# Three reorderings in a fused attention, expert and dense kernel: the order of loads where expert 1 begins, where the weight decoding stands among the experts, and the order of the last sums

## The chip, the cores and the metric

The kernel runs as one program on one core of a Trainium2 chip. The metric is device microseconds per execution; lower is better. Five engines work side by side, each on an instruction stream of its own, strictly in order: TensorE (PE in the profile, with its weight loads as PEld), VectorE (DVE), ScalarE (ACT), GpSimd (POOL) and SyncE (SP). In this kernel nearly all transfers are issued from SP's stream and a few from POOL's; an engine waits for another, or for a transfer, on semaphores.

## The reference

Three stages follow each other. The first is a linear attention with decay over 4 batches, 8 heads and 768 steps; it yields a table `x` of 3072 tokens by 256. The second sends each token to one of 8 experts, and the third is a dense layer pair for all tokens:

```python
expert_idx = np.argmax(logits, axis=1)
for e in range(E):
    mask = expert_idx == e
    h = np.maximum(x[mask] @ w1[e], 0.0)            # 256 -> 1024
    out[mask] = gate_w[mask, None] * (h @ w2[e])    # 1024 -> 256
# third stage, on the experts' output
h = x @ w_in                                        # 256 -> 2048
g = h * np.cos(h)
return (g @ w_out).astype(np.float32)               # 2048 -> 256
```

`w_in` and `w_out` arrive as 64-bit numbers and must be turned into 32-bit ones on the chip.

## The kernel before, in words

**Lists.** While the attention runs, each finished token's row is scattered into a table `xs` in DRAM, behind the rows of its expert's list. A list has room for 432 rows. Behind the last row of list `e`, `fill(e)` (L868) copies a block of zeros `zd` to `xs`, so that a later read of 432 rows finds zeros there and not rubbish. `rows_of(e)` (L879) then reads the list into a tile `xg`. It can be issued only when the zeros of that list have landed.

**Experts.** The loop at L1217 runs over the experts `e` and, inside, over eight slices `f` of the hidden dimension. All products are made in 32-bit precision out of two parts of each operand, a high one and a rest (`h1`, `l1`, `h2`, `l2` of the weights, `xh`, `xl` of the rows, `hh`, `hl` of the hidden values), so that each product takes three matmuls. For each `f`, TensorE makes `ph` (six matmuls, L1233); ScalarE rounds it to `hh` (L1237); VectorE makes the rest `hl` (L1238); and three slices later TensorE takes both up again in `second` (L1201), six matmuls into `py`. So TensorE can run ahead of `hl` by three slices and no further. The last three slices are multiplied after the loop over `f`.

In the same loop stand, in an order that is written out by hand:

- `load_w1(e + 2)` and `load_w2(e + 2)` (L727 and L732): 1 MB each, from SP, into a slot that must be free;
- `split_w(e + 1)` (L756): the high part of the next expert's weights by ScalarE (L743) and the rest by POOL or VectorE (L752), in quarters of 512 columns. `g.S1` names the engine of each quarter for expert 1 alone; later experts use POOL;
- `gates(xg)` (L830) for list `e + 2`: POOL takes a power (L836), VectorE a row of small operations (L840 to L858), and one scaling of the rows (L863, L865);
- `decode()` (L1071): the 64-bit weights of the third stage, 16 pieces of 512 KB fetched one after the other (`fetch`, L1063) into two buffers `raw`. Each piece takes one operation of ScalarE (`tb`, L1084), three of VectorE (L1086, L1088, and L1092 or L1099), and for the first eight pieces one more of each (L1094, L1096). `decode` is a generator; each step of it issues about one operation. `side.take(n)` takes `n` steps: `g.TK[f]` for expert 0 and `g.TE[f]` for the others (L1245), and three more between two experts. At slice 5 of the last expert, all steps that are left are issued at once (L1247);
- `split_out` (L1104): in the last expert, the two parts of `w_out`, by ScalarE and POOL.

**The start of the expert stage.** Between attention and experts a string `g.END` gives the order of the steps that prepare lists 0 and 1. Behind it stand `overflow()` (a branch that isn't taken here), `load_w2(1)`, `fill(2)` from POOL, `rows_of(2)` from SP, and the first two `fetch`es (L1183 to L1188).

**The third stage.** Tokens are taken in blocks `n` (five of 512, two of 256), the 2048 middle columns in 16 slices `f`; a pair (n, f) is a unit. `up` makes `pu`, VectorE and ScalarE make `gh` and `gl` of it, and `down` (L1352), six units later, adds its product to `po` for each 128 tokens `j` of the block. When the last slice of a `j` is in, `finish` (L1316) copies `po` out and scatters the rows to the output, from POOL. In the last block the products of the last two slices are held back and then made for each `j` in turn (L1359 to L1361), so that the first `j` can leave while the second is still computed.

Of the kernel before, what the change touches and what calls it, by code (L numbers as in the profile page):

```python
# [20 lines left out]
NT, D, E, F, F2 = 3072, 256, 8, 1024, 2048  # L21
# [621 lines left out]
def tile_attention_moe_moe2(ctx: ExitStack, tc: tile.TileContext, A1, A2, X, BNh, BT, CT, cst_d, emb, tau, w1, w2, w_in, w_out, out):  # L643
    nc = tc.nc
    ET = mybir.EngineType
    g = G_()
# [33 lines left out]

    g.G1 = (3, 1, 2, 1, 1, 0, 0, 0)
    g.G2 = (0, 0, 0, 0, 2, 0, 2, 2)
    g.TE = (2, 1, 1, 1, 1, 1, 1, 1)
    g.TK = (0, 0, 0, 1, 0, 0, 0, 1)
    g.L2 = "vvvv"
    g.WL = 16
    g.S1 = ("vvvv", "pppp")
    g.WN = {19: 1, 20: 5, 21: 2, 22: 5}
    g.TAIL = "tltttwtwtwmrttttttlrttttwltttttwttwttttttttttt"
    g.END = "wxwcwccwcwwcwwwwwcwxwxwrxxcxxxwwxxxxgxkkgkkggxxxxxg"  # L690
    LAG = 6
    TW = [512] * 5 + [256] * 2
    T0 = [sum(TW[:n]) for n in range(len(TW))]
# [32 lines left out]
    def load_w1(e):  # L726
        r1 = raws[0].tile([128, 2048], F32, tag="r1", name="r1")  # L727
        for k in range(2):
            nc.sync.dma_start(r1[:, F * k:F * k + F], w1[e, 128 * k:128 * k + 128, :])
        W.setdefault(e, {})["r1"] = r1  # L730
# [34 lines left out]
    side = Sides()  # L765
# [102 lines left out]
    def fill(e, et=ET.SP, q=nc.sync):  # L868
        r = nc.values_load(endi[:, e + 1:e + 2], engines=[et], min_val=0, max_val=E * SX - CAP)
        i = q.dma_start(quarters(xs[bass.ds(r, CAP), :]), quarters(zd))  # L870
        for j in prev + early + loads:
            tc.declare_no_dep(i.ins, j, reason="no scatter reaches the rows behind a list's end, and the first list lies before the others")
        return i.ins
# [99 lines left out]
    with ExitStack() as actx:  # L973
        g.apool = actx.enter_context(tc.tile_pool(name="apool", bufs=1))
        g.apool2 = actx.enter_context(tc.tile_pool(name="apool2", bufs=2))
        acc = attn_router(actx, tc, g)

        pcn = g.psU.tile([1, E], F32, tag="u", name="pcn")
        nc.tensor.matmul(pcn, lhsT=g.onesb[:, 0:1], rhs=acc, start=True, stop=True)

        def counts():
            nc.vector.tensor_tensor(out=cnt[:, 1:], in0=pcn, in1=base[:, 1:], op=ALU.subtract)
            yield
            nc.vector.tensor_tensor_scan(out=off, data0=ones[:, :NL], data1=cnt, initial=0.0, op0=ALU.mult, op1=ALU.add)
            yield
            nc.vector.tensor_tensor(out=off, in0=off, in1=cnt, op=ALU.subtract)
            nc.vector.tensor_tensor(out=endi, in0=cnt, in1=base, op=ALU.add)
            fills.append(fill(1, ET.Pool, nc.gpsimd))
            yield
            nc.vector.tensor_copy(cnti, off)  # L990
            xg.append(rows_of(1))

            over = cp.tile([1, NL], F32, name="over")
            nc.vector.tensor_tensor(out=over, in0=cnt, in1=capf, op=ALU.subtract)
            yield
            nc.vector.tensor_scalar(novs, over, 127.0, 0.0, op0=ALU.add, op1=ALU.max)
            yield
            nc.vector.tensor_scalar(novs, novs, 7, None, op0=ALU.arith_shift_right)
            yield
            with nc.allow_low_precision(reason="whole numbers below 2^24"):  # L1000
                nc.vector.tensor_reduce(nov, novs, axis=AX.X, op=ALU.add)

        xg, fills = [], []
        def next_list():
            carved = Carved(few)
            numbers(0, g.xg0, carved)
            yield
            yield from gates(xg[0], carved, g.GE)

        steps = dict(w=g.window, c=counts(), x=second_list(), g=next_list())  # L1010
        for op in g.END:
            if op == "r":
                load_w1(1)
            elif op == "k":
                g.keep_warm(1)
            else:
                next(steps[op], None)
        for op in "xwc":
            for _ in steps[op]:
                pass  # L1020
        xg, = xg
# [8 lines left out]
    with ExitStack() as mctx:  # L1030
# [151 lines left out]

        overflow()  # L1183
        load_w2(1)
        fill(2, ET.Pool, nc.gpsimd)
        xs_ = {1: xg, 2: rows_of(2)}
        numbers(1, xg, mp2, ET.Pool, nc.gpsimd)
        raw_ = [fetch(0), fetch(1)]  # L1188
        x_ = g.x0
        gt = [steps["g"], None]  # L1190
        side.add(decode())
# [25 lines left out]
        for e in range(E):  # L1217
            w = {k: W[e][k].rearrange("p (a b) -> p a b", a=2 if k[1] == "1" else 8) for k in ("h1", "l1", "h2", "l2")}
            xh, xl = x_
            n = wide(e)  # L1220
# [7 lines left out]
            for f in range(8):  # L1228
# [11 lines left out]
                if f >= 3:  # L1240
                    q = f - 3
                    hh, hl = hs.pop(q)
                    for m in range(2):
                        second(py, m, q, w, hh, hl)
                side.take(g.TK[f] if e == 0 else g.TE[f])  # L1245
                if (e, f) == (E - 1, 5):
                    side.drain()  # L1247
                if f == 0 and 0 < e < E - 2:
                    xs_[e + 2] = rows_of(e + 2)
                if f == 2 and e + 3 < E:  # L1250
# [46 lines left out]
    with ExitStack() as zctx:  # L1297
# [30 lines left out]
        NF = F2 // 128  # L1328
# [23 lines left out]
        def down(u):  # L1352

            n, f = units[u]
            nb = TW[n] // 128
            per = 1 if n else 2
            if f == 0:
                PO[n] = [psB.tile([128, 2, D], F32, tag="po", name="po")[:, :per] for _ in range(0, nb, per)]
            last = n == len(TW) - 1 and f >= NF - 2  # L1359

            fs = [] if last and f == NF - 2 else [f - 1, f] if last else [f]  # L1361
            for j in range(nb if fs else 0):
                s = slice(128 * j, 128 * j + 128)
                po, i = PO[n][j // per], j % per
# [17 lines left out]
        for u in range(len(units) + LAG):  # L1382
            ends = LAG <= u < len(units) and units[u - LAG][1] == NF - 1
            if u < len(units):
                n, f = units[u]
# [68 lines left out]
```

## Time and profile before

| | |
|---|---|
| runs | 586.79, 586.77, 585.42 us; median 586.77 us |
| the profiled execution | 587.23 us, of which the span from its first to its last instruction is 585.6 us |
| TensorE's granted clock, mean over the span | 0.978 |
| busy | PE 94%, DVE 76%, POOL 54%, ACT 51% |
| the chain that ended last | PE 56%, DVE 8%, transfers 4%, POOL 3%, ACT 2% |

The attention ends near 140 us, the experts run from there to 306 us, and the third stage from there to the end. A busy TensorE is not TensorE at its peak, since matmuls overlap and their ends are modelled; idle time of another engine costs nothing by itself.

### The profile page before, as it was taken

The numbers are of one execution on the slowest core, as the hardware profiler recorded it, in microseconds if no ns is written. First come the engines' busy times: TensorE is split into PE (matmuls) and PEld (weight loads), VectorE is DVE, ScalarE is ACT, GpSimd is POOL, SyncE is SP. The second block draws the span as 40 slices with busy tenths as digits, with TensorE's granted clock in tenths as the row PEclk, the third lists the DMA queues.
The fourth block names the chain that finished last, engine by engine and source line by source line (L and its number), as shares of the span: only waits on it lengthen the run. The fifth ranks groups of instructions, "written<-read, shape, count | busy, mean of one in ns | idle before, by whom it ended". The sixth has DMA issues, their size and how long they took to land.

```text
span 585.6 us, 11047 instructions
## 1 busy us (share of the span) xinstructions
PE 551.4 (94%) x4000; PEld 502.1 (86%) x4000; DVE 443.3 (76%) x876; ACT 297.6 (51%) x637; POOL 314.1 (54%) x345
## 2 busy tenths in 40 slices
PE   7698999979789999999979999999999999999994
PEld 5587887878788999989968999999999999999994
DVE  5899999847787998787648977767777677776882
ACT  5163533534457566657554645445446445445562
POOL 4323543462456584566633746746745745845763
PEclk9899999999989999999979999999999999999998
DMA  8899895127676665752211000100100100100000
GB/s 202 221 218 220 206 244 166 40 93 224 232 180 240 195 194 179 244 171 81 72 37 1 2 1 1 36 2 1 38 0 1 38 1 1 38 1 9 30 20 18
DMA packets 28993, 57.00 MB, mean 97 GB/s; under 512 B 7216, under 2 KB 16056, under 8 KB 28184
## 3 DMA queue, kind: packets, MB, share of 16 engines
q1 hardware_dynamic: 26184, 47.77, 29.2%
q0 software_dynamic: 2752, 8.51, 4.4%
q8 instruction: 32, 0.52, 0.4%
q14 instruction: 25, 0.20, 0.1%
HBM read 48.50 MB, written 11.07 MB: 102 GB/s over the span
## 4 chain that ended last, share of the span: by engine, by line
PE 56%; DVE 8%; DMA 4%; POOL 3%; issue 3%; ACT 2%; POOLq 0%; SPq 0%; ACTq 0%; DVEq 0%
PE po L1373 22%; PE pu L1339 22%; PE ph L1233 6%; PE py L1203 6%; DMA xg<-xs 2%; DVE hl L1238 2%; POOL gl L1410 1%; POOL l L752 1%; DVE lg L840 1%; DVE xg L863 1%; DVE ta L1092 1%; DVE ta L1088 1%; ACT hh L1237 1%; DMA r<-in_w 1%; DMA raw<-in_w_out 1%
## 5 line engine op out<-in xcount | busy, mean ns | idle before, releaser
L1410 POOL TENSOR_TENSOR gl<-gg,gh 128x512 fp32r<-128x512 f32 (+1 forms) x111 | 125.9, 1140 | 106.4 <-PE pu L1339 63.2
L1400 ACT ACTIVATE cc<-ff,half 128x512 f32<-128x512 f32 (+1 forms) x112 | 74.4, 665 | 129.2 <-DVE ff L1398 123.3
L1396 DVE TENSOR_SCALAR tt<-pu 128x512 f32<-128x512 f32 (+1 forms) x110 | 67.4, 613 | 64.9 <-PE pu L1339 62.3
L1373 PE MATMUL po<-h,gl 128*128 128x256 f32 x384 | 108.2, 282 | 0.0
L1373 PE MATMUL po<-l,gh 128*128 128x256 f32 x384 | 108.2, 282 | 0.0
L1373 PE MATMUL po<-h,gh 128*128 128x256 f32 x382 | 107.6, 282 | 0.0
L752 POOL TENSOR_TENSOR l<-r,h 128x512 fp32r<-128x512 f32 x52 | 72.4, 1406 | 45.5 <-ACT h L743 45.1
L1373 PEld LDWEIGHTS po<-h,gh 128*128 128x128 f32 x382 | 72.3, 189 | 3.6
L1373 PEld LDWEIGHTS po<-l,gh 128*128 128x128 f32 x384 | 72.6, 189 | 3.1
L1373 PEld LDWEIGHTS po<-h,gl 128*128 128x128 f32 x384 | 73.0, 190 | 0.1
L1398 DVE SCALAR_TENSOR_TENSOR ff<-tt,pu 128x512 f32<-128x512 f32 (+1 forms) x110 | 67.0, 609 | 3.8
L1339 PE MATMUL pu<-yh,il 128*128 128x512 f32 (+1 forms) x192 | 68.5, 357 | 0.0
L1339 PE MATMUL pu<-yh,ih 128*128 128x512 f32 (+1 forms) x192 | 68.2, 355 | 0.0
L1339 PE MATMUL pu<-yl,ih 128*128 128x512 f32 (+1 forms) x192 | 68.0, 354 | 0.0
L1406 DVE SCALAR_TENSOR_TENSOR gg<-pu,cc 128x512 f32<-128x512 f32 (+1 forms) x110 | 66.7, 606 | 0.4 <-ACT cc L1400 0.4
L1409 ACT CAST gh<-gg 128x512 fp32r<-128x512 f32 (+1 forms) x112 | 60.9, 544 | 0.4 <-DVE gg L1406 0.3
L1238 DVE SCALAR_TENSOR_TENSOR hl<-ph,hh 128x432 fp32r<-128x432 f32 (+1 forms) x64 | 36.7, 577 | 24.0 <-ACT hh L1237 23.9
L1203 PE MATMUL py<-hl,h 128*128 128x432 f32 (+1 forms) x128 | 46.5, 363 | 7.8 <-DVE hl L1238 7.7
L1203 PE MATMUL py<-hh,h 128*128 128x432 f32 (+1 forms) x128 | 45.8, 358 | 2.1 <-ACT hh L1237 2.1
L1237 ACT ACTIVATE hh<-ph 128x432 fp32r<-128x432 f32 (+1 forms) x64 | 32.8, 512 | 27.8 <-PE ph L1233 27.5
L1203 PE MATMUL py<-hh,l 128*128 128x432 f32 (+1 forms) x128 | 46.0, 359 | 0.0
L1233 PE MATMUL ph<-xl,h 128*128 128x432 f32 x112 | 40.7, 363 | 0.8 <-DVE xl L1055 0.8
(220 smaller groups left out, 1205.6 us busy)
## 6 DMA issues: line engine op xcount, KB each, us to landing
r<-in_w SPq DMA_DIRECT2D x32, 512.0 KB
ac<-acd SPq DMA_DIRECT2D x10, 512.0 KB
raw<-in_w_in SPq DMA_DIRECT2D x8, 512.0 KB
raw<-in_w_out SPq DMA_DIRECT2D x8, 512.0 KB
xg<-xs SPq DMA_DIRECT2D x7, 462.4 KB
xs<-zd SPq DMA_DIRECT2D x5, 462.4 KB
XB<-in_X SPq DMA_DIRECT2D x8, 256.0 KB
bt<-in_BT SPq DMA_DIRECT2D x6, 256.0 KB
```

The lines of the kernel that those rows point to most:

```text
L752: (nc.vector if engines[q] == "v" else nc.gpsimd).tensor_tensor(out=l[:, s], in0=W[e][rn][:, s], in1=h[:, s].bitcast(F32), op=ALU.subtract)
L1203: nc.tensor.matmul(py[m][:, :b_.shape[1]], lhsT=a_[:, q, 128 * m:128 * m + 128], rhs=b_, start=q == 0 and k == 0, stop=q == 7 and k == 2)
L1233: nc.tensor.matmul(ph[:, :n], lhsT=a_[:, c, 128 * f:128 * f + 128], rhs=b_[:, c], start=k == 0, stop=k == 5)
L1238: nc.vector.scalar_tensor_tensor(out=hl, in0=ph[:, :n], scalar=0.0, in1=hh.bitcast(F32), op0=ALU.max, op1=ALU.subtract)
L1339: nc.tensor.matmul(PU[u], lhsT=a_[:, c, 128 * f:128 * f + 128], rhs=b_[:, c], start=c == 0 and k == 0, stop=c == 1 and k == 2)
L1373: nc.tensor.matmul(po[:, i], lhsT=a_[:, s], rhs=b_, start=first and per == 1, stop=q == NF - 1 and k == 2 and i == per - 1)
L1396: nc.vector.tensor_scalar(tt, pu, 0.25, MAGIC, op0=ALU.add, op1=ALU.add)
L1398: nc.vector.scalar_tensor_tensor(out=ff, in0=tt, scalar=-MAGIC, in1=pu, op0=ALU.add, op1=ALU.subtract)
L1400: nc.scalar.activation(cc, ff, AF.Sin, bias=half, scale=-TWO_PI)
L1406: nc.vector.scalar_tensor_tensor(out=gg, in0=pu, scalar=TWO_PI, in1=cc, op0=ALU.mult, op1=ALU.mult)
L1409: nc.scalar.copy(gh, gg)
L1410: (nc.vector if u >= len(units) else nc.gpsimd).tensor_tensor(out=gl, in0=gg, in1=gh.bitcast(F32), op=ALU.subtract)
```

## The change

It has five edits. `fill(2)` moves from behind `overflow()` and `load_w2(1)` to a place inside the string `g.END` (the new letter `f`), still on POOL. The first two `fetch`es move ahead of `rows_of(2)`. Two of the four quarters of `l2` of expert 1 go from POOL to VectorE (`g.S1`). The steps of `decode` are given for each expert: as before in experts 0 to 4, three more in expert 5, seven more in expert 6, two per slice in expert 7, and no drain at slice 5. In the last block of the third stage, four slices are held back, and no longer two.

```diff
-    g.TE = (2, 1, 1, 1, 1, 1, 1, 1)
-    g.TK = (0, 0, 0, 1, 0, 0, 0, 1)
+
+    g.TE = [(0, 0, 0, 1, 0, 0, 0, 1)] + [(2, 1, 1, 1, 1, 1, 1, 1)] * 4 + [(2, 2, 1, 1, 2, 1, 1, 2)] + [(2, 2, 2, 2, 2, 2, 2, 2)] * 2
     g.L2 = "vvvv"
     g.WL = 16
-    g.S1 = ("vvvv", "pppp")
+    g.S1 = ("vvvv", "vpvp")
...
-    g.END = "wxwcwccwcwwcwwwwwcwxwxwrxxcxxxwwxxxxgxkkgkkggxxxxxg"
+    g.END = "wxwcwccwcwwcwwwwwcwxwxwrxxfcxxxwwxxxxgxkkgkkggxxxxxg"
...
+            elif op == "f":
+                fills.append(fill(2, ET.Pool, nc.gpsimd))
...
         overflow()
         load_w2(1)
-        fill(2, ET.Pool, nc.gpsimd)
+        raw_ = [fetch(0), fetch(1)]
         xs_ = {1: xg, 2: rows_of(2)}
         numbers(1, xg, mp2, ET.Pool, nc.gpsimd)
-        raw_ = [fetch(0), fetch(1)]
...
-                side.take(g.TK[f] if e == 0 else g.TE[f])
-                if (e, f) == (E - 1, 5):
-                    side.drain()
+                side.take(g.TE[e][f])
...
-            last = n == len(TW) - 1 and f >= NF - 2
+            last = n == len(TW) - 1 and f >= NF - 4
 
-            fs = [] if last and f == NF - 2 else [f - 1, f] if last else [f]
+            fs = [] if last and f < NF - 1 else [f - 3, f - 2, f - 1, f] if last else [f]
```

SP's stream where the expert stage begins, before (`r` is `w2` of expert 1, `xg` the rows of list 2, `raw` the 64-bit weights, `zd` the zeros that `fill(3)` copies, and the last `r` is `w1` of expert 2):

```order
L735 DMA r_2282<-in_w 128x4x256 x2
L883 DMA xg<-xs 108x1096
L1066 DMA raw<-in_w_in 128x1024 x2
L870 DMA xs<-zd 16x7398
L729 DMA r_2418<-in_w 128x1024 x2
```

The same place in the changed kernel:

```order
L735 DMA r_2293<-in_w 128x4x256 x2
L1068 DMA raw<-in_w_in 128x1024 x2
L883 DMA xg<-xs 108x1096
L870 DMA xs<-zd 16x7398
L729 DMA r_2418<-in_w 128x1024 x2
```

The two pieces of 64-bit weights now stand ahead of the rows of list 2, and nothing else in this stream moved.

VectorE's stream from the end of expert 0 to the first `hl` of expert 1, before (`lg` to `r` and `dl` are the gates of list 2, `ta` the first decoded piece; rows of 128x256 are expert 0's):

```order
L1238 SCALAR_TENSOR_TENSOR hl<-ph,hh 128x256 x2
L1055 TENSOR_TENSOR xl<-px,xh 128x864
L1238 SCALAR_TENSOR_TENSOR hl<-ph,hh 128x256
L840 TENSOR_TENSOR lg<-xg 108x32
L842 TENSOR_REDUCE mx<-lg 108x4
L844 TENSOR_TENSOR lg<-lg,mx 108x32
L846 TENSOR_SCALAR r<-r 108x4
L848 RECIPROCAL r<-r 108x4
L850 TENSOR_TENSOR dl<-lg,r 108x32
L1086 TENSOR_SCALAR ta<-tb 128x512
L1088 SCALAR_TENSOR_TENSOR ta<-tb,ta 128x512
L1092 SCALAR_TENSOR_TENSOR ta<-raw,ta 128x512
```

The same stretch after (its first row stands between the first two `hl` of the rows above):

```order
L752 TENSOR_TENSOR l_2468<-r_2293,h_2466 128x512
L1239 SCALAR_TENSOR_TENSOR hl<-ph,hh 128x256
L1057 TENSOR_TENSOR xl<-px,xh 128x864
L1239 SCALAR_TENSOR_TENSOR hl<-ph,hh 128x256
L840 TENSOR_TENSOR lg<-xg 108x32
L842 TENSOR_REDUCE mx<-lg 108x4
L844 TENSOR_TENSOR lg<-lg,mx 108x32
L846 TENSOR_SCALAR r<-r 108x4
L848 RECIPROCAL r<-r 108x4
L752 TENSOR_TENSOR l_2468<-r_2293,h_2466 128x512
L850 TENSOR_TENSOR dl<-lg,r 108x32
L1088 TENSOR_SCALAR ta<-tb 128x512
```

Two quarters of `l2` of expert 1 have come in, one before the rows of list 2 are needed and one behind them.

VectorE's stream in the last expert from its fourth `hl`, before (`wof` is the decoded `w_out`; the last two `hl` are those of slices 6 and 7):

```order
L1238 SCALAR_TENSOR_TENSOR hl<-ph,hh 128x432 x3
L1086 TENSOR_SCALAR ta<-tb 128x512
L1088 SCALAR_TENSOR_TENSOR ta<-tb,ta 128x512
L1099 SCALAR_TENSOR_TENSOR wof<-raw,ta 128x512
L1086 TENSOR_SCALAR ta<-tb 128x512
L1088 SCALAR_TENSOR_TENSOR ta<-tb,ta 128x512
L1099 SCALAR_TENSOR_TENSOR wof<-raw,ta 128x512
L1086 TENSOR_SCALAR ta<-tb 128x512
L1088 SCALAR_TENSOR_TENSOR ta<-tb,ta 128x512
L1099 SCALAR_TENSOR_TENSOR wof<-raw,ta 128x512
L1238 SCALAR_TENSOR_TENSOR hl<-ph,hh 128x432 x2
```

The whole of the last expert after:

```order
L1239 SCALAR_TENSOR_TENSOR hl<-ph,hh 128x432
L1088 TENSOR_SCALAR ta<-tb 128x512
L1239 SCALAR_TENSOR_TENSOR hl<-ph,hh 128x432
L1090 SCALAR_TENSOR_TENSOR ta<-tb,ta 128x512
L1101 SCALAR_TENSOR_TENSOR wof<-raw,ta 128x512
L1239 SCALAR_TENSOR_TENSOR hl<-ph,hh 128x432 x2
L1088 TENSOR_SCALAR ta<-tb 128x512
L1090 SCALAR_TENSOR_TENSOR ta<-tb,ta 128x512
L1239 SCALAR_TENSOR_TENSOR hl<-ph,hh 128x432
L1101 SCALAR_TENSOR_TENSOR wof<-raw,ta 128x512
L1239 SCALAR_TENSOR_TENSOR hl<-ph,hh 128x432 x3
```

Of the nine decoding operations ahead of `hl` 6 and 7 none is left there. Expert 7 has six in all, spread ahead of its sixth `hl`; before it had twelve. The other six stand in experts 5 and 6.

## Rows read from the trace of the kernel before

**Rows 1.** Stages, windows view: length, busy of PE, PEld, DVE, ACT, POOL, clock.

```profile
117.00:140.30 23.30, 19.05 (x180) 17.76 (x176) 13.20 (x59) 8.06 (x23) 11.34 (x21) 1.00 0.44 148
160.00:182.00 22.00, 18.44 (x87) 16.87 (x88) 18.08 (x33) 12.52 (x25) 12.18 (x11) 0.84 0.69 196
240.60:261.00 20.40, 19.44 (x104) 18.30 (x103) 17.09 (x27) 12.55 (x25) 12.48 (x10) 1.00 0.54 180
261.00:281.00 20.00, 20.00 (x108) 19.20 (x108) 14.87 (x23) 12.02 (x25) 11.67 (x8) 1.00 0.31 104
281.00:306.30 25.30, 21.65 (x97) 20.03 (x96) 14.15 (x22) 13.58 (x25) 11.89 (x8) 0.88 0.19 63
```

**Rows 2.** PE, timeline: a wait in the attention, and one in expert 1.

```profile
123.87 0.73 PE L252 MATMUL pt<-IE,yT 128*128 128x136 f32 x4 [2.22 <-ACT yT L242]
...
163.08 0.73 PE L1203 MATMUL py<-hl,h 128*128 128x432 f32 x1 [4.74 <-DVE hl L1238]
```

**Rows 3.** DVE, timeline: the gates of list 2 and the first `hl` of expert 1.

```profile
153.94 0.19 DVE L840 TENSOR_TENSOR lg<-xg 108x32 f32<-108x32 f32 x1 [3.07 <-DMA xg<-xs]
...
154.39 5.81 DVE L844 TENSOR_TENSOR lg<-lg,mx 108x32 f32<-108x32 f32 x1
...
162.43 0.60 DVE L1238 SCALAR_TENSOR_TENSOR hl<-ph,hh 128x432 fp32r<-128x432 f32 x1
```

**Rows 4.** POOL, timeline: list 1's power, `fill(2)`, and expert 1's `l2`.

```profile
137.50 1.13 POOL L836 TENSOR_TENSOR few<-xg,pw 108x4 f32<-108x4 f32 x1 [1.90 <-DMA xg<-xs]
140.08 0.58 POOL L870 DMA_DIRECT2D xs<-zd  x1 [1.46 <-SPq L1121]
...
155.17 4.98 POOL L752 TENSOR_TENSOR l<-r,h 128x512 fp32r<-128x512 f32 x4
```

**Rows 5.** ACT, timeline: the first decoding operation.

```profile
155.16 0.67 ACT L1084 ACTIVATE tb<-raw 128x512 f32<-128x512 f32 x1 [4.78 <-DMA raw<-in_w_in]
```

**Rows 6.** SP, timeline of issues: expert 1's start, and expert 4's (`fill` follows its rows).

```profile
139.41 0.95 SPq L735 DMA_DIRECT2D r<-in_w  x2
149.52 0.37 SPq L883 DMA_DIRECT2D xg<-xs  x1
...
160.18 0.95 SPq L735 DMA_DIRECT2D r<-in_w  x2
...
199.75 0.93 SPq L735 DMA_DIRECT2D r<-in_w  x2
...
209.26 0.55 SPq L870 DMA_DIRECT2D xs<-zd  x1
```

**Rows 7.** Chain that ended last, in order of time: start, length, what.

```profile
161.24 9.09 DMA xg<-xs
...
280.92 4.67 PE ph L1233 x24
...
293.43 3.27 DMA raw<-in_w_out
...
300.90 5.41 PE py L1203 x14
```

**Rows 8.** PE, timeline: its two waits in the last expert.

```profile
298.45 0.47 PE L1203 MATMUL py<-hh,h 128*128 128x432 f32 x1 [1.67 <-ACT hh L1237]
300.90 0.73 PE L1203 MATMUL py<-hl,h 128*128 128x432 f32 x1 [1.98 <-DVE hl L1238]
```

**Rows 9.** Last block: PE, then DVE's last `gl`, then POOL's scatters.

```profile
574.69 0.28 PE L1373 MATMUL po<-h,gh 128*128 128x256 f32 x1
...
577.45 0.28 PE L1373 MATMUL po<-h,gl 128*128 128x256 f32 x1
...
575.27 0.43 DVE L1410 TENSOR_TENSOR gl<-gg,gh 128x256 fp32r<-128x256 f32 x1 [0.53 <-ACT gh L1409]
...
577.70 0.99 POOL L1321 DMA_INDIRECT out<-so,pidx  x1 [2.37 <-ACT so L1318]
...
578.99 0.96 POOL L1321 DMA_INDIRECT out<-so,pidx  x1 [0.21 <-issue]
```

## The prediction, made before the changed kernel was run

> **What bounds the kernel now.** I read the stages first, then TensorE's waits, then the chain of waits at these places, and last the streams of the engines that are waited for. In a plain expert stretch TensorE is busy for all of its time (20.00 of 20.00 us from 261 us on) at the full granted clock. Two stretches fall out of this: the one from 160 us with a granted clock of 0.84, and the last expert's, with 0.88 and 21.65 of 25.30 us busy [rows 1]. TensorE's longest waits of the expert stage lie there too: 4.74 us in expert 1 [rows 2], and 1.67 and 1.98 us in expert 7 [rows 8].
>
> **Place A, the start of expert 1.** SP issues `w2` of expert 1 at 139.41 us and the rows of list 2 only at 149.52 [rows 6], because the zeros behind that list, issued by POOL at 140.08, must land first [rows 4]. The rows are there at 153.94, when VectorE's `lg` ends its wait for them [rows 3]. The first piece of 64-bit weights, issued behind the rows, lets ScalarE go on at 155.16, after 4.78 us of idling [rows 5]. On VectorE the reader should see one row: the subtraction of L844, as small as the 0.19 us sum before it, takes 5.81 us and ends at 160.20 [rows 3]. POOL's run of four quarters of `l2` ends at 160.15 [rows 4]. So VectorE stands still until POOL's run is over. From there to the end of the first `hl` of expert 1 (162.43 plus 0.60) are 2.83 us, and 0.05 us later TensorE goes on. The clock adds to it: 0.84 over 22.00 us means 7.0 us at the 1.2 GHz level; 3.1 us of these TensorE was still waiting, and of the other 3.9 it lost half, 1.95 us. Place A costs 4.74 + 1.95 = 6.7 us.
>
> **Place B, expert 7.** It runs from 280.92 to 306.31 (300.90 plus 5.41), 25.4 us. Its 96 matmuls at the pace of its first 24 (4.67 us [rows 7]) take 18.7. The 6.7 us between are the two waits (3.65) and the clock (0.12 of 25.30, 3.0). The cause stands in the chain: the last piece of 64-bit weights is issued at 293.43, lands 3.27 us later [rows 7], and the decoding behind it stands ahead of the last two `hl` on VectorE.
>
> **The change, part by part.** Times are for the profiled execution, 587.23 us with its 585.6 us of span.
>
> **Zeros earlier.** The zeros of list 2 may not overwrite what the read of list 1 still takes, so POOL can issue them when list 1's rows are in, at 137.50, where its power now starts [rows 4]: 2.6 us earlier. Queued behind them on POOL are a copy and the power of list 1, which start later by 0.8 us (0.58 of issue [rows 4] and some 0.2 of address). SP's store of list 1's numbers waits for the copy, so `w2` moves from 139.41 to 140.3. I cost the delay at nothing, since expert 0's own work covers it; without that cover it is 0.8 us. The zeros took 9.4 us; if they take as long again, they land at 146.9.
>
> **Raw weights ahead of the rows.** ScalarE's 4.78 us of idling goes. But the rows now stand behind 2 MB instead of 1. The nearest row is expert 4's start, with `w2`, one piece, rows in this order: issued from 199.75, all in by 209.26 [rows 6], 9.5 us for 2.0 MB. With a second piece it is 2.5 MB, or 11.9 us, and the rows of list 2 land at T = 152.2 instead of 153.94. Bounds: 149.8 if the second piece costs nothing; 156.0 if the zeros land at 146.9 and the rows then take the 9.09 us that those of list 3 took [rows 7]. I take 152.2, because it comes from the same mix of transfers.
>
> **Two quarters to VectorE.** POOL's run after the rows is then a power (1.13 [rows 4]), a small copy (0.2) and two quarters of 1.25: 3.8 us, where it was 6.2. The first quarter on VectorE hides in its 3.07 us of idling before `lg` [rows 3]. The second stands on the path and costs 0.7 (an `hl` of 432 columns takes 0.60 [rows 3]; this one has 512). So `hl` ends at T + 3.8 + 0.7 + 2.83 = 159.5, and TensorE goes on 3.5 us earlier than at 163.08. What is left of its wait, which began at 158.3, is about 1.2 us, or 1.7 since ScalarE no longer holds back the matmul before it. The nearest wait in size, 2.22 us [rows 2], lies in a stretch with clock 1.00 [rows 1], so I take it that the clock stays and the 1.95 us come back too: 5.4 us. What is late next are the rows of list 3. They stand behind `w2` of expert 2, which SP could issue at 160.18 [rows 6], when the last quarter freed its slot. Now it is freed at T + 4.9 = 157.1, 3.1 us earlier, with less in flight. Expert 2 can follow by 3.1 us or a little more, where TensorE could by 5.4. I take **-4.5** for place A; the bounds are 0 (the rows land at T = 156, so that `hl` ends as late as before) and -6.7 (all that place A costs).
>
> The Trainium skill, page "SBUF — State Buffer", section "Who interferes with whom", says that a VectorE instruction with two SBUF inputs and a GpSimd instruction that reads SBUF exclude each other, and that the one that issues second is blocked until the first finishes. The row agrees that they exclude each other and differs in the length: the 5.81 us reach over five POOL instructions or more, not to the end of one. By the page's wording the subtraction would be free after the power, 1.1 us behind the rows, and place A would gain all 6.7 us.
>
> **Decoding spread.** It takes nine VectorE operations and the wait for a transfer out of place B: 6.7 us. Late next is the first block of the third stage, whose parts ScalarE makes from `py` while TensorE does its last nine matmuls, now at full clock (1.8 us, no longer 3.3); I leave 0.3 us for it, so **-6.4**. In return experts 5 and 6 get about two and four of VectorE's operations of 0.4 to 0.7 us, 3.9 us at most. VectorE was busy for 17.09 of 20.40 us in expert 5 and 14.87 of 20.00 in expert 6 [rows 1], so it stays below the length of an expert, and `hl` has three slices of leeway, but some operations will stand behind a POOL run. Between 0 and 3.9 I take **+0.5**, near the low end because expert 6, which gets most, had the most room.
>
> **Last sums.** The last 24 matmuls, 0.12 us apart, run from 574.69 to 577.45. The first 128 tokens now leave six matmuls earlier, by 0.72 us, and their scatter no longer holds up the second one on POOL, which began at 578.99; it can begin 0.72 us after the old start of the first, 577.70 + 0.72 = 578.42 [rows 9]. The new order needs the last `gl` at the twelfth matmul, 576.0, and it is ready at 575.70. So **-0.55**; if `gl` came late it would be 0.
>
> Sum: -4.5 - 6.4 + 0.5 - 0.55 = -10.95, and 587.23 becomes 576.3. The profiled execution stood 0.46 us above the median of the runs (586.77), so I predict 575.8.
>
> **The rivals.**
> 1. The forecast, 573.5 to 578.5: 0.53.
> 2. The rows of list 2 come no earlier. For it: 2 MB in front of them. T near 154 leaves TensorE about 3 us of waiting, and the clock falls as it did after 3.65 us in expert 7. Place A then gives 1 us: 579 to 580.5. Chance 0.20.
> 3. VectorE becomes the bound in experts 5 and 6: the 3.9 us arrive whole, with waits for POOL on top: 579 to 582.5. Against it: the free 3.3 and 5.1 us of these stretches. Chance 0.11.
> 4. The lock ends with one instruction: place A gives 6.7: 573.6 or a little less. The 5.81 us over a whole run speak against it, and nothing in this trace for it; I keep it because one row is all that shows the long lock. Chance 0.08. The Trainium skill's page "SBUF — State Buffer", section "Who interferes with whom", speaks for it.
> 5. Slower. If the rows sink far behind the raw weights, place A loses what place B and the end give (6.45 us). That takes T + 7.3 = 163.1 + 6.45, so T = 162.2: 22 us for 2.5 MB. At T = 164.5 it is 589. Expert 4's 2.0 MB in 9.5 us speak against it. Chance 0.04. The Trainium skill, page "DMA: Bandwidth & Descriptors", section "Queues, rings and completion order", says that a queue's descriptors are consumed in ring order on each DMA engine, so rows issued last cannot pass the raw weights.
> 6. The change does not do what it says: the pieces are held by their buffers as before, at both places: within 0.3%. The streams of the changed kernel speak against it. Chance 0.04.
>
> Cases 1 to 4 are faster by more than 0.3% (1.8 us, about what a measurement of this kernel can tell from no change): 0.92. Same 0.04, slower 0.04. The range 572.5 to 581.0 holds cases 1 and 4, nearly all of 2 and half of 3: somewhat over 8 in 10.
>
> **What would show each step.** Right: SP's rows of list 2 land near 152; the subtraction of L844 takes about 3.5 us; TensorE's wait in expert 1 is under 2.5 us with no stretch at 1.2 GHz; expert 7 lasts under 19.5 us without a wait over 0.5; experts 5 and 6 keep 19.5 to 21 us; POOL's last two scatters lie 1.3 us apart or more. The prediction is wrong if the rows land after 154, if the clock falls at 160 us all the same, or if expert 5 or 6 grows by more than 1.5 us.

## The result and the profile after

The changed kernel takes 579.88 us (median of 6 runs, 577.19 to 581.36) against 585.7 for the kernel before (6 runs): ratio 0.9894, 95% interval 0.9865 to 0.9924. It is faster by some 6 us, where 11 were forecast; the time lies in the range, near its upper end.

The windows view by stage, of the changed kernel (columns as in [rows 1]):

```profile
140.30:160.00 19.70, 15.40 (x96) 14.11 (x94) 12.92 (x24) 8.35 (x19) 4.35 (x5) 0.91 0.66 206
160.00:182.00 22.00, 20.12 (x87) 18.12 (x88) 15.27 (x26) 12.20 (x26) 11.97 (x10) 0.85 0.72 196
...
260.00:282.00 22.00, 20.32 (x107) 19.01 (x106) 20.16 (x32) 13.54 (x27) 11.51 (x9) 1.00 0.42 144
282.00:300.50 18.50, 18.50 (x96) 17.75 (x95) 11.46 (x16) 12.28 (x23) 11.95 (x8) 1.00 0.09 29
```

The last expert (282 us on) is now a plain stretch: TensorE busy throughout, at full clock, where it was 0.88 before [rows 1]. The stretch from 160 us is as it was, with a granted clock of 0.85 (0.84 before). So place B came back and place A did not.

TensorE's timeline at the places of the prediction: the first matmul of expert 0, one near its end, the waits in expert 1, the first of expert 2, the start of expert 6, and the last matmul of all.

```profile
135.97 0.58 PE L1234 MATMUL ph<-il,h 128*128 128x256 f32 x2 [1.21 <-ACTq L1123]
...
149.97 0.41 PE L1204 MATMUL py<-hh,l 128*128 128x256 f32 x1
...
160.16 0.73 PE L1204 MATMUL py<-hl,h 128*128 128x432 f32 x1 [3.23 <-DVE hl L1239]
...
176.05 0.46 PE L1204 MATMUL py<-hh,h 128*128 128x432 f32 x1 [1.20 <-ACT hh L1238]
...
180.50 0.35 PE L1234 MATMUL ph<-xh,h 128*128 128x432 f32 x1
...
261.89 0.47 PE L1234 MATMUL ph<-xl,h 128*128 128x432 f32 x1 [1.55 <-DVE xl L1057]
...
571.58 0.28 PE L1372 MATMUL po<-h,gl 128*128 128x256 f32 x1
```

Expert 1's wait is 3.23 us and no longer 4.74 [rows 2], but expert 2 starts at 180.50, 44.5 us after expert 0's first matmul; before it was 39.7. That the two absolute times are alike is an accident: the attention, which the edits hardly touch, ended 4.4 us sooner in this execution (135.97, where the kernel before has 140.33). In the profiles of this study expert 0 begins anywhere from 135.6 to 141.4 us, so places are compared below by their distance from that matmul, and kernels by their timed ratios. The chip has a part in this: in the four profiles of one chip it begins at 138.8 to 141.4 us, in the six of two others at 135.6 to 137.5.

VectorE, timeline: the gates of list 2, the first `hl` of expert 1, and the landing of list 3's rows with what follows.

```profile
152.99 0.19 DVE L840 TENSOR_TENSOR lg<-xg 108x32 f32<-108x32 f32 x1 [4.10 <-DMA xg<-xs]
...
153.44 3.37 DVE L844 TENSOR_TENSOR lg<-lg,mx 108x32 f32<-108x32 f32 x1
...
159.50 0.60 DVE L1239 SCALAR_TENSOR_TENSOR hl<-ph,hh 128x432 fp32r<-128x432 f32 x1
...
169.30 0.19 DVE L840 TENSOR_TENSOR lg<-xg 108x32 f32<-108x32 f32 x1 [2.02 <-DMA xg<-xs]
169.41 0.60 DVE L1239 SCALAR_TENSOR_TENSOR hl<-ph,hh 128x432 fp32r<-128x432 f32 x1
169.92 3.69 DVE L1094 SCALAR_TENSOR_TENSOR ta<-raw,ta 128x512 uint32<-128x512 uint32 x1
```

GpSimd, timeline: the zeros and the copy behind them, the quarters of `l2` of expert 1, and the work behind list 3's rows.

```profile
135.02 0.57 POOL L870 DMA_DIRECT2D xs<-zd  x1 [2.82 <-DMA xg<-xs]
135.60 0.20 POOL L826 COPY few<-xg 128x2 f32<-128x2 f32 x1
...
154.22 2.54 POOL L752 TENSOR_TENSOR l<-r,h 128x512 fp32r<-128x512 f32 x2
...
169.41 1.00 POOL L836 TENSOR_TENSOR r<-xg,pw 108x4 f32<-108x4 f32 x1 [3.39 <-DMA xg<-xs]
170.37 0.19 POOL L826 COPY ic<-xg 108x4 f32<-108x4 f32 x1
170.51 2.55 POOL L752 TENSOR_TENSOR l<-r,h 128x512 fp32r<-128x512 f32 x2
```

SP, timeline of issues: `w2` of expert 1, the raw pieces, the rows of list 2; later `w2` of expert 2 and the rows of list 3.

```profile
137.81 1.35 SPq L735 DMA_DIRECT2D r<-in_w  x2
139.21 1.72 SPq L1068 DMA_DIRECT2D raw<-in_w_in  x2
141.22 1.49 SPq L883 DMA_DIRECT2D xg<-xs  x1
...
157.76 0.96 SPq L735 DMA_DIRECT2D r<-in_w  x2
158.83 0.57 SPq L883 DMA_DIRECT2D xg<-xs  x1
```

What the reader is to see: the rows of list 2 are issued at 141.22, right after the raw pieces, and land 11.8 us later (152.99); before, they were issued ahead of the raw pieces and took 4.4 us (149.52 to 153.94, [rows 3, 6]). The subtraction of L844 is shorter, 3.37 us for 5.81. Then the same happens once more with list 3: VectorE waits for its rows, GpSimd begins a run when they land, and VectorE's L1094 takes 3.69 us, until that run is over. TensorE's 1.20 us wait before expert 2 lies behind it.

### The profile page after: what moved, and what is told of

It is laid out like the page before. It is cut to its first block, busy times and chain, and to the rows that moved or that the text cites. A ratio compares the mean times of both kernels' runs of the same rounds, so it can differ in the third digit from the quotient of the medians.

```text
span 579.1 us, 11037 instructions
## 1 busy us (share of the span) xinstructions
PE 552.6 (95%) x4000; PEld 502.0 (87%) x4000; DVE 444.9 (77%) x878; ACT 298.0 (51%) x637; POOL 310.5 (54%) x343
## 4 chain that ended last, share of the span: by engine, by line
PE 57%; DVE 9%; DMA 4%; issue 2%; ACT 2%; POOL 1%; POOLq 0%; SPq 0%; ACTq 0%
PE po L1372 22%; PE pu L1338 22%; PE py L1204 6%; PE ph L1234 6%; DMA xg<-xs 4%; DVE hl L1239 2%; DVE ta L1090 2%; DVE xg L863 1%; POOL gl L1409 1%; DVE ta L1094 1%; ACT hh L1238 1%; DVE lg L844 1%; DVE lg L840 1%; DVE ta L1088 1%; DVE wof L1101 1%
## 5 line engine op out<-in xcount | busy, mean ns | idle before, releaser
L752 POOL TENSOR_TENSOR l<-r,h 128x512 fp32r<-128x512 f32 x50 | 69.5, 1406 | 48.7 <-ACT h L743 48.3
```

The lines of the kernel that those rows point to most:

```text
L752: (nc.vector if engines[q] == "v" else nc.gpsimd).tensor_tensor(out=l[:, s], in0=W[e][rn][:, s], in1=h[:, s].bitcast(F32), op=ALU.subtract)
```

## The experiments

Each kernel was timed beside the kernel before on the same chip. Beside the changed kernel itself (median before 585.7 us) there are three groups on different chips: "start alone" to "list 3 sooner" (median before 585.13 us), "zeros behind the copy" to "rows first, zeros back" (588.14), and the last two (584.67). So ratios are compared; a ratio need not equal the quotient of the two medians. Two ratios whose intervals reach 0.003 to either side differ clearly only from about 0.004 (2.3 us) on, an estimate from these intervals. Distances are from the one profiled execution of each, and they differ by chance too: "start alone" and the changed kernel have the same start and lie 2.4 us apart at rows 2, 2.9 us at expert 2. In this table, "rows 2" and "rows 3" are the landings of those lists after expert 0's first matmul, "expert 2" is its first matmul after the same point.

| kernel | median us | ratio, 95% interval | rows 2 | rows 3 | expert 2 |
|---|---|---|---|---|---|
| before | | 1 | 13.6 | 30.0 | 39.7 |
| changed | 579.88 | 0.9894 (0.9865 to 0.9924) | 17.0 | 33.3 | 44.5 |
| start alone | 583.54 | 0.9992 (0.9971 to 1.0013) | 14.6 | 30.5 | 41.6 |
| spread alone | 579.39 | 0.9903 (0.9880 to 0.9927) | 14.3 | 29.9 | 40.6 |
| rows first | 576.01 | 0.9845 (0.9817 to 0.9873) | 13.2 | 28.1 | 39.0 |
| list 3 sooner | 576.28 | 0.9858 (0.9833 to 0.9883) | 15.4 | 26.5 | 40.1 |
| zeros behind the copy | 582.22 | 0.9906 (0.9879 to 0.9933) | 14.0 | 30.2 | 39.8 |
| rows first, quarters back | 579.22 | 0.9863 (0.9837 to 0.9890) | 12.1 | 27.3 | 38.4 |
| three edits | 576.42 | 0.9816 (0.9790 to 0.9842) | 13.5 | 24.1 | 37.1 |
| rows first, zeros back | 581.94 | 0.9896 (0.9873 to 0.9920) | 15.2 | 30.4 | 40.1 |
| expert 2's quarters | 576.32 | 0.9864 (0.9837 to 0.9891) | 15.2 | 31.7 | 39.5 |
| three edits, wider spread | 573.47 | 0.9811 (0.9785 to 0.9837) | 12.4 | 25.2 | 36.1 |

The theory at the outset ("pinned"): the start's three edits gain nothing, because the rows of list 2 now stand behind 1 MB of raw weights, and because expert 2 is released by the landing of list 3's rows. Its rivals: the gain was there and the profiled execution hid it; or something else than the rows (VectorE's work, the clock) holds expert 2.

**Start alone.** The kernel before with these edits and no others:

```diff
-    g.S1 = ("vvvv", "pppp")
+    g.S1 = ("vvvv", "vpvp")
...
-    g.END = "wxwcwccwcwwcwwwwwcwxwxwrxxcxxxwwxxxxgxkkgkkggxxxxxg"
+    g.END = "wxwcwccwcwwcwwwwwcwxwxwrxxfcxxxwwxxxxgxkkgkkggxxxxxg"
...
+            elif op == "f":
+                fills.append(fill(2, ET.Pool, nc.gpsimd))
...
-        fill(2, ET.Pool, nc.gpsimd)
+        raw_ = [fetch(0), fetch(1)]
         xs_ = {1: xg, 2: rows_of(2)}
         numbers(1, xg, mp2, ET.Pool, nc.gpsimd)
-        raw_ = [fetch(0), fetch(1)]
```

> The kernel before with the three edits at the start of expert 1 alone (zeros earlier, raw weights ahead of the rows, two quarters to VectorE). Theory 'pinned' (the rows of list 2 now stand behind two raw pieces, and expert 2 is released by the landing of list 3's rows, which follows from it): no gain, between 1 us faster and 4 us slower than before (585 to 590 us); the rows of list 2 land 16 us or more after expert 0's first matmul, 13.6 before. Rival 'hidden by chance' (the edits gain what was forecast, the one profiled execution only does not show it): 4.5 us faster, about 581.

0.9992: no gain (at most 1.7 us by the interval), so the one profiled execution did not hide a gain of the forecast size. The rows of list 2 land 14.6 us after expert 0's first matmul; "16 or more" was too much for this execution, but they are not sooner than before.

**Spread alone.** The kernel before with the new table and without the drain:

```diff
-    g.TE = (2, 1, 1, 1, 1, 1, 1, 1)
-    g.TK = (0, 0, 0, 1, 0, 0, 0, 1)
+    g.TE = [(0, 0, 0, 1, 0, 0, 0, 1)] + [(2, 1, 1, 1, 1, 1, 1, 1)] * 4 + [(2, 2, 1, 1, 2, 1, 1, 2)] + [(2, 2, 2, 2, 2, 2, 2, 2)] * 2
...
-                if (e, f) == (E - 1, 5):
-                    side.drain()
```

> The kernel before with the decoding spread alone. Theory 'pinned': this edit carries nearly the whole gain, 5 to 6 us (ratio 0.990 to 0.9915): expert 7 under 19.5 us instead of 25.4, experts 5 and 6 together 1 us longer. Rival 'hidden by chance': part of the gain of the changed kernel is the start's, so here it is under 3 us.

0.9903, 5.7 us (4.3 to 7.0 by the interval): this edit carries the gain. Expert 7 takes 18.8 us there as in the changed kernel.

**Rows first.** The changed kernel, with the raw pieces behind the rows again:

```diff
         load_w2(1)
-        raw_ = [fetch(0), fetch(1)]
         xs_ = {1: xg, 2: rows_of(2)}
         numbers(1, xg, mp2, ET.Pool, nc.gpsimd)
+        raw_ = [fetch(0), fetch(1)]
```

> The changed kernel with the first two raw pieces put back behind the rows of list 2; the zeros stay early and the quarters stay on VectorE. Theory 'pinned': the rows of list 2 land about 13 us after expert 0's first matmul or sooner (17.0 in the changed kernel), those of list 3 about 3 us sooner with them, and the time is 2 to 4 us below the changed kernel. Rival 'ScalarE' (the raw pieces behind the rows hold ScalarE up as they did before): TensorE waits in expert 1 as long as before and the time equals the changed kernel's within 1 us. Rival 'hidden by chance': 1 to 3 us slower than the changed kernel.

0.9845 against 0.9894, a ratio lower by 0.005 or 2.9 us; the intervals overlap by a hair. Rows 2 land 13.2 us after expert 0's first matmul, rows 3 at 28.1. ScalarE's idling for the first raw piece is back (2.97 us, 4.78 before [rows 5]), and it does not decide: TensorE waits 1.47 us in expert 1, and the rival "ScalarE" falls.

What the order changes can be seen at the DMA engines. These are the last 3 us before the rows of list 2 land, in the changed kernel and then in this one (the last two columns are the DMA engines' busy share and GB/s):

```profile
149.97:152.97 3.00, 3.00 (x11) 2.83 (x11) 0.00 (x0) 2.03 (x5) 0.00 (x0) 0.50 0.07 26
```

```profile
147.65:150.65 3.00, 2.35 (x16) 1.78 (x15) 1.76 (x4) 1.17 (x4) 0.00 (x0) 1.00 0.99 282
```

In the same 3 us the share is 0.31 to 0.41 in the four other kernels that have the raw pieces ahead of the rows, and 0.79 to 0.96 in the six others that have the rows ahead. When the rows are the last in the queue, nothing fills the time of their last packets, since the zeros of list 3 and the loads behind them go out only when the rows are in. That this idle transfer time is what the order costs is argued here and not tested by itself.

The subtraction of L844 showed something not looked for. VectorE's and GpSimd's timelines of this kernel:

```profile
151.12 2.12 DVE L844 TENSOR_TENSOR lg<-lg,mx 108x32 f32<-108x32 f32 x1
```

```profile
150.73 1.04 POOL L836 TENSOR_TENSOR r<-xg,pw 108x4 f32<-108x4 f32 x1 [5.89 <-DMA xg<-xs]
151.74 0.18 POOL L826 COPY ic<-xg 108x4 f32<-108x4 f32 x1
151.89 1.29 POOL L752 TENSOR_TENSOR l<-r,h 128x512 fp32r<-128x512 f32 x1
153.56 1.71 POOL L752 TENSOR_TENSOR l<-r,h 128x512 fp32r<-128x512 f32 x1 [0.38 <-ACT h L743]
```

GpSimd's first gap comes after one quarter (at 153.18, where it waits 0.38 us for ScalarE), and there VectorE goes on (153.24).

**List 3 sooner.** The changed kernel with `w2` of expert 2 behind the rows of list 3:

```diff
                     xs_[e + 2] = rows_of(e + 2)
+                    if e == 1:
+                        load_w2(2)
...
-            if e + 2 < E:
+            if 0 < e < E - 2:
                 load_w2(e + 2)
```

> The changed kernel with one edit: the rows of list 3 are issued ahead of w2 of expert 2 and no longer behind it. Theory 'pinned': they land 16 to 17 us or less after w1 of expert 2 is issued becomes about 8, that is some 5 us sooner relative to the landing of list 2's rows (16.3 us behind them in the changed kernel, here 10 to 12); expert 2 starts sooner and the time falls by 2 to 4 us. Rival 'VectorE' (the work of expert 1 on VectorE, with its locks by GpSimd, sets the start of expert 2, whenever the rows land): the rows land sooner and the time stays within 1 us. Rival 'clock' (TensorE's falls to 1.2 GHz took the gain back): expert 2's start moves by less than 1 us and the clock still falls twice.

0.9858. Rows 3 land 11.1 us after rows 2 (16.3 in the changed kernel), and the time is lower by about 2 us (0.0036), as forecast, but the intervals overlap. By distances expert 2 starts 4.4 us sooner than in the changed kernel's profile. VectorE no longer waits for the rows, and L1094 takes 1.26 us; but the run that the rows set off on GpSimd now meets the operation ahead of it:

```profile
165.38 2.37 DVE L1090 SCALAR_TENSOR_TENSOR ta<-tb,ta 128x512 uint32<-128x512 uint32 x1
...
168.29 1.26 DVE L1094 SCALAR_TENSOR_TENSOR ta<-raw,ta 128x512 uint32<-128x512 uint32 x1
```

The clock fell once, at the 4.16 us wait in expert 1, and expert 2 started sooner all the same. That speaks against the rivals "VectorE" and "clock"; the difference in time is too small to rule them out.

**Zeros behind the copy.** A new question: in the changed kernel `w2` goes out 1.84 us after expert 0's first matmul, in the kernel before 0.92 ahead of it, since the copy that SP's store needs is queued on GpSimd behind the zeros, which wait for list 1's rows. One letter of the string moves:

```diff
-    g.END = "wxwcwccwcwwcwwwwwcwxwxwrxxfcxxxwwxxxxgxkkgkkggxxxxxg"
+    g.END = "wxwcwccwcwwcwwwwwcwxwxwrxxcxxxwwxxxxgfxkkgkkggxxxxxg"
```

> The changed kernel with the zeros of list 2 one step later in GpSimd's stream: behind the copy of list 0's numbers and no longer ahead of it. Theory 'delay' (the zeros wait on GpSimd for list 1's rows, the copy behind them is held up, SP's store waits for the copy, and w2 of expert 1 with all that follows it on SP goes out late): w2 goes out about 2.5 us sooner, 0.6 us ahead of expert 0's first matmul instead of 1.8 us behind it; the rows of list 2 land 1.5 to 2.5 us sooner, and the time is 1 to 2.5 us below the changed kernel's 579.9. Rival 'raw weights alone' (expert 0's own work covers the delay, only the two raw pieces ahead of the rows cost): w2 sooner, the time within 0.7 us of the changed kernel's.

`w2` is issued 0.9 us ahead, as expected, and the rows of list 2 land 3 us sooner than in the changed kernel's profile (14.0 and 17.0). Yet the ratio is 0.9906, no gain over 0.9894 and as the rival said. "Delay" falls, and a distance of one profile is seen not to be a gain in time. With `w2` issued only 0.8 us behind them (2.8 in the changed kernel) the zeros themselves take 7.5 us, 6.1 in the changed kernel, so part of what `w2` wins the zeros lose.

**Rows first, quarters back.** The kernel "rows first" with the four quarters on GpSimd:

```diff
-    g.S1 = ("vvvv", "vpvp")
+    g.S1 = ("vvvv", "pppp")
```

> The kernel with the rows of list 2 first (raw pieces behind them; 576.0) and the four quarters of l2 of expert 1 back on GpSimd. If VectorE is locked out for the whole of GpSimd's run: the subtraction of L844 takes 4 us or more (2.1 in the kernel with the rows first, 3.4 in the changed one), TensorE waits 3 us or more in expert 1 (1.5), the slot of w2 of expert 2 comes free some 2 us later, the rows of list 3 land later by the same, and the time is 1.5 to 3 us longer, 577.5 to 579. If the lock lasts one instruction of GpSimd only: L844 under 1.5 us and no change. If the quarters lie beside other waits: longer lock, but within 0.7 us of 576.0.

VectorE's L844 and GpSimd's run in its timelines:

```profile
152.83 5.85 DVE L844 TENSOR_TENSOR lg<-lg,mx 108x32 f32<-108x32 f32 x1
```

```profile
153.60 5.03 POOL L752 TENSOR_TENSOR l<-r,h 128x512 fp32r<-128x512 f32 x4
```

The lock is as long as before (5.85 us), and TensorE waits 4.02 us in expert 1. Yet expert 2 starts 38.4 us after expert 0's first matmul, no later than in "rows first" (39.0), although the rows of list 2 landed 1.1 us sooner here, so that from their landing it is 0.5 us later. By ratio the kernel is 0.0018 or 1 us slower, inside both intervals, where 1.5 to 3 us were expected of the longer lock. So a wait of 4 us in expert 1 that ends before list 3's rows are in costs far less than its length; whether it costs nothing can't be told.

**Three edits.** "Rows first", "zeros behind the copy" and "list 3 sooner" together:

> The changed kernel with three edits together: the raw pieces behind the rows of list 2, the zeros behind the copy, the rows of list 3 ahead of w2 of expert 2. If each loss at the start is one of its own: 573.5 to 575, the fastest of all. If they are the same loss (expert 2 is then released by VectorE's work in expert 1, whenever rows land): 575.5 to 576.5, as with one of the edits.

0.9816, 1.7 us below "rows first", within the intervals; expert 2 starts at 37.1, earlier than with any one of the edits. Put on the chip of "rows first" (0.9816 of 585.13) it is 574.4 us, in the range of the first alternative, but too near to the second to tell them apart.

**Rows first, zeros back.** "Rows first" with `fill(2)` behind `load_w2(1)`, as before the change:

```diff
-    g.END = "wxwcwccwcwwcwwwwwcwxwxwrxxfcxxxwwxxxxgxkkgkkggxxxxxg"
+    g.END = "wxwcwccwcwwcwwwwwcwxwxwrxxcxxxwwxxxxgxkkgkkggxxxxxg"
...
+        fill(2, ET.Pool, nc.gpsimd)
         xs_ = {1: xg, 2: rows_of(2)}
```

> The kernel with the rows of list 2 first (576.0) and the zeros of list 2 back at their old place, behind w2 of expert 1. If the early zeros are worth what brings the rows sooner: the rows of list 2 land 14.3 us after expert 0's first matmul as before (13.2 with early zeros) and the time is about 1 us longer, 577. If the held-up copy costs as much as the early zeros bring: the same within 0.7 us.

0.9896, 3 us above "rows first" and more than the 1 us expected; the same as the changed kernel. Early zeros with the raw pieces ahead of the rows gain nothing, late zeros with the rows ahead gain nothing, the two together 3 us. The intervals touch at 0.9873. A second pair, both with four quarters on GpSimd, goes the same way: "rows first, quarters back" is 0.0040 below "spread alone", 2.3 us, of which the last sums, which "spread alone" leaves as before, are some 0.6.

**Expert 2's quarters.** The changed kernel, with the two quarters that GpSimd makes behind list 3's power moved to VectorE:

```diff
-g.S1[int(part) - 1] if e == 1 else "pppp")
+g.S1[int(part) - 1] if e == 1 else ("pppv", "vppp")[int(part) - 1] if e == 2 else "pppp")
```

> The changed kernel with the two quarters of expert 2's rests that stand behind list 3's power on GpSimd moved to VectorE. If it is GpSimd's run behind the landing of list 3's rows that holds the start of expert 2 (VectorE's L1094 takes 3.7 us there in the changed kernel and in every other kernel in which VectorE waits for those rows): L1094 takes 0.7 to 1.9 us, expert 2 starts 9 to 10 us behind the landing of list 3's rows (11.2 in the changed kernel, 10.7 to 11.1 in three others), and the time falls by 1 to 1.5 us. If the rows themselves and the work behind them on VectorE hold it: the lock is gone, but the 11 us stay within 0.5, and the time too.

VectorE's timeline of this kernel behind list 3's rows:

```profile
167.42 0.19 DVE L840 TENSOR_TENSOR lg<-xg 108x32 f32<-108x32 f32 x1 [2.32 <-DMA xg<-xs]
167.53 0.69 DVE L752 TENSOR_TENSOR l<-r,h 128x512 fp32r<-128x512 f32 x1
...
168.65 0.69 DVE L1094 SCALAR_TENSOR_TENSOR ta<-raw,ta 128x512 uint32<-128x512 uint32 x1
```

L1094 takes 0.69 us and no longer 3.69. Expert 2 starts 7.8 us behind the rows (11.2 in the changed kernel). The changed kernel spends the 3.4 us between the two figures in three waits of TensorE (0.34, 1.20 and 0.18 us) and in a clock of 0.66 over 5.00 us, 1.7 us lost; here TensorE neither waits nor slows down between the landing and expert 2. The changed kernel's row:

```profile
176.00:181.00 5.00, 4.77 (x15) 4.20 (x16) 3.93 (x7) 2.41 (x5) 3.16 (x3) 0.66 0.63 233
```

So the profile bears out the first alternative: in the changed kernel list 3's rows hold expert 2 by the run that they set off on GpSimd. The ratio is 0.9864, 0.003 or 1.8 us lower as expected, but the intervals overlap, and the gain in time is not shown.

**Three edits, wider spread.** The fastest kernel so far, with the decoding spread over experts 4 to 7:

```diff
-[(2, 1, 1, 1, 1, 1, 1, 1)] * 4 + [(2, 2, 1, 1, 2, 1, 1, 2)] + [(2, 2, 2, 2, 2, 2, 2, 2)] * 2
+[(2, 1, 1, 1, 1, 1, 1, 1)] * 3 + [(2, 2, 1, 1, 2, 1, 1, 2)] * 2 + [(2, 2, 2, 1, 2, 1, 1, 2)] + [(2, 2, 2, 2, 2, 2, 2, 2)]
```

> The kernel with three edits at the start (raw pieces behind the rows of list 2, zeros behind the copy, rows of list 3 ahead of w2 of expert 2; ratio 0.9816 to the kernel before), with the decoding spread wider: three more steps in expert 4, three in expert 5 as before, four instead of seven in expert 6. If VectorE's operations make expert 6 longer (21.7 us in the changed kernel, 19.5 before): expert 6 takes 20 to 20.5 us, experts 4 to 6 together are 0.5 to 1 us shorter, ratio 0.980 to 0.981. If it is only a wait of expert 5 that has moved to expert 6: experts 4 to 6 together within 0.3 us, no difference in time.

Expert 6 takes 19.5 us, less than the 20 to 20.5 expected, but expert 5 21.0 (19.6 in "three edits"): together experts 4 to 6 are 0.7 us shorter, and the ratio, 0.9811, can't be told from 0.9816. Mostly a wait has moved from one expert to the next. It and "three edits" beat both kernels, by some 11 us and 4.5 to 5 us.

## Why the prediction was half right

- **Decoding spread, forecast -6.4 and +0.5: right.** Expert 7 took 25.4 us and takes 18.8 (281.85 to 300.67 in the chain of waits), -6.6. Experts 5 and 6 together grew from 40.3 to 41.3 us, +0.9. One wait stands behind it: 1.55 us for `xl` at the start of expert 6 (261.89 above). Ahead of that `xl` VectorE made two decoding operations that took 1.51 and 1.66 us beside GpSimd's quarters (their rows stand in the last section), where the same two took 0.42 and 0.69 us at 160.64 in the kernel before, with GpSimd idle. "Spread alone" confirms the sum, 5.7 us. But "expert 6, which gets most, had the most room" did not hold: expert 6 grew by 2.2 us, beyond the 1.5 that was to be a sign of being wrong, and only because expert 5 lost a wait and 1.2 us does the sum come out near +0.5.

```profile
281.85 4.67 PE ph L1234 x24
...
295.94 4.73 PE py L1204 x24
300.67 1.46 PE pu L1338 x6
```

- **Last sums, forecast -0.55: right.** From the last matmul to the end of the span were 8.15 us [rows 9] (585.6 less 577.45); now they are 579.1 less 571.58, 7.5. That is -0.6. The scatters start 1.44 us apart (1.29 before), and the second begins 0.97 us after the last matmul. All nine profiles with this edit end 7.5 to 7.6 us after that matmul, the three without it 8.1 to 8.2; no run times the edit alone.

The scatters now:

```profile
571.11 0.98 POOL L1320 DMA_INDIRECT out<-so,pidx  x1 [1.65 <-ACT so L1317]
...
572.55 0.96 POOL L1320 DMA_INDIRECT out<-so,pidx  x1 [0.36 <-ACT so L1317]
```

- **Place A, forecast -4.5: wrong, and this is the step that failed.** The three edits are worth 0.5 us, between -1.7 and +0.8 us by the interval of "start alone". Three links of the step broke. First, "the rows of list 2 land at T = 152.2", 11.9 us after `w2` and the same after expert 0's first matmul (140.33): measured after `w2` in the four profiles with the changed kernel's order there (its own, "start alone", "list 3 sooner" and "expert 2's quarters"), it took 15.2, 12.7, 13.6 and 13.4 us; with `w2` itself going out 1.7 to 1.9 us later than forecast, the rows landed 14.6 to 17.0 us after that matmul. The landing at 152.99 looks like the forecast 152.2 only because the attention ended 4.4 us sooner. Expert 4's start, from which the 11.9 came, was no measure for this place: the zeros are still on their way here until the rows go out at 141.22, and the estimate by bytes has no term for the last microseconds, in which the DMA engines were nearly idle. Second, "I take it that the clock stays": it fell at the 3.23 us wait, as in the kernel before at 4.74 (the prediction had named this fall as a sign of being wrong), and also at the end of expert 0 and before expert 2. Third, "expert 2 can follow by 3.1 us or a little more": list 3's rows were named as late next, and rightly, but only their issue was followed. SP did issue `w2` of expert 2 sooner, 4.8 us after the rows of list 2 had landed (6.2 before), and the rows of list 3 landed 16.3 us after those of list 2 all the same (16.4 before). They land 30.5 us after expert 0's first matmul in "start alone" and 33.3 in the changed kernel, against 30.0 before.
- **What went right in it.** The lock was shortened as worked out: L844 took 3.37 us, "about 3.5" was written. It bought little, since by the profiles its end did not decide when expert 2 starts ("rows first, quarters back": 1 us in time, not told from nothing).
- **The rivals.** What came true is the second, rows no earlier and a clock that falls: 579 to 580.5 was its time, and it had a chance of 0.20. That the time fell into the stated range is owed to this rival, which the range took in; the forecast itself, 575.8, missed by 4 us, nearly all of it at place A. Of the third only the wait in expert 6 came, +0.9 us in all and not 3.9. The fourth (the lock ends with one instruction) is refuted by the lengths of L844 in the last section. The fifth needed T = 162.2 and was far off; the rows did land behind the raw pieces that were issued ahead of them in all five profiles with that order (in the changed kernel the first piece lets ScalarE go on at 149.76), which shows their order and not that they can't pass.

Where the gain went, then: the early zeros are worth 2 to 3 us once the rows follow at once. The raw pieces ahead of the rows take these away again. What an earlier end of the lock leaves is, by the profiles, lost before expert 2: in the changed kernel TensorE goes on 7.2 us after the rows of list 2 land (160.16 and 152.99), in the kernel before 9.1 us, but the lock behind list 3's rows, which was there before too, cost it no wait then and 1.7 us of waits now. The kernel before:

```profile
170.97 3.68 DVE L1092 SCALAR_TENSOR_TENSOR ta<-raw,ta 128x512 uint32<-128x512 uint32 x1
```

What stays open is how much of the remaining loss in expert 1 belongs to the clock: it fell in all of these kernels but the fastest, and no experiment took it away alone. Nor can the share of each of the three links be told apart from single profiles.

## What to carry to other kernels

When a wait is shortened, follow the transfers that start behind it to their landing, not to their issue: where each list's rows must land before the next list's zeros and rows can go, the last landing can set the start of the next stage, and a wait that ends before it then costs little. Two transfers that are each moved ahead can cancel; test the pair, not only the sum. And one profiled execution can differ from the next by more than the edit under study (here up to 5.8 us in the stage before between chips, up to 2.7 on one), so set distances from a common point beside timed ratios.

## What the hardware showed beyond the expected

The small subtraction of L844 took 5.81 us before and 5.85 in "rows first, quarters back" (four quarters in a row on GpSimd), 3.37 in the changed kernel (two in a row), and 2.12 in "rows first" (one, then a gap of 0.38 us). In each case it ended within 0.1 us of GpSimd's first gap. So this operation, which reads two tiles, stands still for an unbroken run of GpSimd's instructions, and a gap of 0.38 us frees it. An operation that reads one tile came through sooner: in the changed kernel L1088 begins beside the first of two quarters that follow each other without a gap and is done at 258.91, when the second still runs to 260.05; L1090 behind it, which reads two, ends at 260.60:

```profile
257.32 2.73 POOL L752 TENSOR_TENSOR l<-r,h 128x512 fp32r<-128x512 f32 x2 [0.41 <-ACT h L743]
```

```profile
257.40 1.51 DVE L1088 TENSOR_SCALAR ta<-tb 128x512 uint32<-128x512 uint32 x1
258.94 1.66 DVE L1090 SCALAR_TENSOR_TENSOR ta<-tb,ta 128x512 uint32<-128x512 uint32 x1
```

The Trainium skill, page "SBUF — State Buffer", section "Who interferes with whom", has the engine that issues second blocked until the other's instruction is over; the runs here agree that the two exclude each other, and for operations that read two tiles they show a longer block.

TensorE's clock fell in the changed kernel also where no wait was over 0.6 us: at the end of expert 0 TensorE was busy for 1.77 of 3.00 us, its two longest waits were 0.58 us each, and its next matmuls ran at the 1.2 GHz level (0.41 us each at 149.97; the same shape takes 0.28 us at 571.58), as the windows view shows:

```profile
146.00:149.00 3.00, 1.77 (x11) 1.14 (x9) 2.41 (x4) 1.94 (x5) 0.00 (x0) 1.00 0.83 235
149.00:153.00 4.00, 4.00 (x18) 3.82 (x19) 0.01 (x1) 2.24 (x5) 0.00 (x0) 0.59 0.15 54
```
